# Gate functions and products ranked ahead of weight conversions, and six low-word conversions on GpSimd

## The chip, the cores and the metric

The kernel runs on one core of a Trainium2 chip. The metric is the device time of one execution in microseconds (us), the median of several runs. The engines are PE (TensorE matmuls), PEld (its weight loads), DVE (VectorE), ACT (ScalarE), POOL (GpSimd) and SP (SyncE, which here issues DMAs); each executes its own queue of instructions strictly in order, and engines wait for each other by semaphores.

## The reference

Two stages in float32. First a linear recurrence over 768 steps for 4 batches and 8 heads of size 48, then a feed-forward network over the 3072 tokens with 384 channels and 2048 hidden units, whose gate is Mish:

```python
def _attn_ref(r, k, v, w, u):
    for t in range(S):
        cur = np.einsum('bhd,bhe->bhde', u[None] * kt, vt)
        y[:, :, t] = np.einsum('bhd,bhde->bhe', rt, state + cur)
        state = w[None, :, :, None] * state + np.einsum('bhd,bhe->bhde', kt, vt)

def _moe_ref(x, w_in, w_out):
    h = x @ w_in
    sp = np.where(h > 20.0, h, np.log1p(np.exp(np.minimum(h, 20.0))))
    g = h * np.tanh(sp)
    return g @ w_out
```

The recurrence's output, with heads side by side, is x. The two weights arrive as 64-bit floats and have to be turned into 32-bit ones on the chip.

## The kernel before

**Work and tiles.** The recurrence is computed in 24 steps (s = 0 to 23), each a chunk of 64 time steps for two batches. A step scales its r and k (L484, L540), forms scores on PE (L555), masks them with `copy_predicated` (L595), multiplies with v (L608, or L621 in later steps) and keeps a state (L663, copied out by L679). A step yields one slice of x, 128 tokens wide: for the first steps it is transposed on PE (L750), copied out of PSUM by ACT (L719), and from group 1 on a rest is taken by DVE (L722).

The feed-forward network goes over 8 groups of three slices (384 tokens). In each group there are 16 hidden tiles of 128 units, 0 to 15. A tile has an up product (`hp`), which is copied out of PSUM to `hb` (L918), a gate, and a down product into three accumulators (`acc`). Four tiles form a batch for the gate. Its functions work on all four tiles at once on ACT: sigmoid (L835), arctan (L838) and sine (L841), the first and the last behind a load of a function table (ACT_TABLE_LOAD). The products with `hb` follow on DVE in two halves (L850). Group 0 uses whole float32 weights (L811, L824, L869); from group 1 on x, gate and weights are each split into a rounded part and a rest, with three matmuls for one (L777; L853 and L856 split the gate, L384 and L386 the weights).

**Weights.** Each of the two weights arrives in eight loads of 768 KB, numbered 0 to 15 in the order of use (`W_ORDER`). Load 7, for instance, holds the up weights of tiles 10 and 11, load 9 those of tiles 12 and 13, load 10 the down weights of tiles 6 and 7. A load is converted in place once, in group 0's time: its low words are turned into a small float by `convert_low` (L341, ACT); its high words go through an absolute value (L358 on ACT or L360 on DVE), a clamp (L362), a shift (L364), a merge with the sign (L367) and an integer add of both words (L369), which ends the conversion (event `whole`). The buffer `we` between them has two slots.

**What sets the order.** All of this is written as generators ("threads") that yield the engines that could do the next operation with an estimated price, or the name of an event to wait for. The planner `Flow.run` takes at each step the engine and the thread that can start first by these estimates, and among those that can start at the same time the one of the lowest rank. The instructions are then issued in just this order (`manual_schedule`), so each engine's queue is fixed at build time. Ranks are counted in hidden tiles: a thread that belongs to tile n has the rank n minus a lead. The leads are the constants `L_...`: L_IN and L_OUT for conversions of up and down weights, L_GATE for a gate's functions and the halves of its product, L_FIN for a slice's way into x. The recurrence's first steps have ranks far below all others. In the first 30 us PE gets dummy matmuls (L285) to keep its clock up.

## Time and profile before

| | us |
|---|---|
| median of 3 runs | 525.7 |
| lowest, highest run | 525.6, 526.51 |
| profiled execution, its own time | 524.44 |
| span of the profile (first to last instruction) | 522.7 |
| busy in the span: PE, PEld | 506.4, 468.7 |
| busy in the span: ACT, DVE, GpSimd | 402.3, 321.4, 10.1 |
| mean granted TensorE clock | 0.994 |

A row of the profile gives the line, the engine, the operation and the tiles written and read (out<-in), with busy time, mean time of one instruction in nanoseconds, and the idle time ahead of it with its cause. In the order of time the first two columns are start and length in us. A group's float32 matmul of the whole weights counts as two instructions.

### The profile page before, as it was taken

How to read it: one execution, taken by the hardware profiler on the slowest of the kernel's cores; microseconds unless marked ns; L12 is line 12 of the kernel's file. 1: busy time of each engine (PE TensorE's matmuls, PEld its weight loads, DVE VectorE, ACT ScalarE, POOL GpSimd, SP SyncE). 2: the span in 40 equal slices, each digit the busy share in tenths (PEclk: the TensorE clock that was granted, in tenths of full speed). 3: DMA queues.
4: the chain of work that ended last, by engine and by line, in shares of the span. 5: the costliest groups of instructions: out<-in, count | busy, mean ns of one | idle time of the engine just before them, and what ended most of it. 6: DMA issues, size and time to landing. Idle time of an engine off the chain costs nothing.

```text
span 522.7 us, 11439 instructions
## 1 busy us (share of the span) xinstructions
PE 506.4 (97%) x4757; PEld 468.7 (90%) x4757; DVE 321.4 (62%) x486; ACT 402.3 (77%) x505; POOL 10.1 (2%) x23
## 2 busy tenths in 40 slices
PE   8797999999999999999999999999999999999994
PEld 6674666788999999999999999999999999999994
DVE  7989889857775475565564475575474473334341
ACT  6889985968988778667787678667687767777883
POOL 7000000000000000000000000000000000000000
PEclk9998999999999999999999999999999999999998
DMA  8998444323333343423533343413343240001001
GB/s 256 415 376 266 113 117 119 95 56 107 90 110 107 96 141 100 113 63 93 148 91 87 98 134 100 107 52 105 113 126 96 70 153 15 2 1 45 2 0 51
DMA packets 31051, 57.88 MB, mean 111 GB/s; under 512 B 6064, under 2 KB 19248, under 8 KB 30992
## 3 DMA queue, kind: packets, MB, share of 16 engines
q1 hardware_dynamic: 27536, 52.32, 34.1%
q10 hardware_dynamic: 3456, 4.75, 2.6%
q8 instruction: 39, 0.64, 0.5%
q14 instruction: 20, 0.16, 0.1%
HBM read 36.80 MB, written 4.72 MB: 79 GB/s over the span
## 4 chain that ended last, share of the span: by engine, by line
PE 84%; ACT 6%; DVE 3%; DMA 2%; issue 2%; SPq 2%; ACTq 0%
PE hp L777 30%; PE acc L777 28%; PE acc L869 6%; PE pa L555 5%; PE hp L824 5%; PE yt L621 3%; PE st L663 3%; PE yt L608 1%; SPq L742 1%; PE hp L811 1%; ACT L841 1%; ACT fa L841 1%; ACT fa L838 1%; DMA rk<-in_rkT_dram 1%; DVE rk L484 1%
## 5 line engine op out<-in xcount | busy, mean ns | idle before, releaser
L777 PE MATMUL hp<-x,w 128*128 128x384 f32 x1008 | 197.2, 338 | 0.5 <-DMA x<-rkn 0.5
L777 PE MATMUL acc<-gh,w 128*128 128x384 f32 x672 | 187.9, 335 | 1.0 <-ACT gh L853 1.0
L777 PEld LDWEIGHTS hp<-x,w 128*128 128x128 f32 x1008 | 175.7, 188 | 3.7 <-issue 0.7
L777 PEld LDWEIGHTS acc<-gh,w 128*128 128x128 f32 x672 | 122.8, 188 | 1.4 <-ACT gh L853 1.3
L777 PE MATMUL acc<-gl,w 128*128 128x384 f32 x336 | 112.3, 334 | 0.2 <-DVE gl L856 0.2
L918 ACT COPY hb<-hp 128x384 f32<-128x384 f32 x104 | 49.2, 474 | 55.5 <-PE hp L777 47.2
L850 DVE TENSOR_TENSOR hb<-hb,fa 128x768 f32<-128x768 f32 (+1 forms) x58 | 51.8, 927 | 41.0 <-ACT fa L841 40.9
L853 ACT CAST gh<-hb 128x768 fp32r<-128x768 f32 (+1 forms) x58 | 47.2, 816 | 22.2 <-DVE hb L850 22.0
L777 PEld LDWEIGHTS acc<-gl,w 128*128 128x128 f32 x336 | 63.1, 188 | 0.4 <-DVE gl L856 0.4
L918 DVE COPY hb<-hp 128x384 f32<-128x384 f32 x24 | 13.4, 556 | 77.6 <-PE hp L777 77.4
L856 DVE TENSOR_TENSOR gl<-hb,gh 128x768 fp32r<-128x768 f32 (+1 forms) x58 | 52.7, 929 | 7.7 <-ACT gh L853 5.9
L835 ACT ACTIVATE fa<-hb,bias_ln 128x1536 f32<-128x1536 f32 (+1 forms) x33 | 50.9, 1542 | 0.4
L838 ACT ACTIVATE fa<-fa 128x1536 f32<-128x1536 f32 (+1 forms) x33 | 47.8, 1449 | 1.9 <-ACT ob L881 1.7
L841 ACT ACTIVATE fa<-fa 128x1536 f32<-128x1536 f32 (+1 forms) x33 | 47.8, 1448 | 0.4
L841 ACT ACT_TABLE_LOAD x33 | 42.3, 1283 | 0.6
L835 ACT ACT_TABLE_LOAD x33 | 42.3, 1283 | 0.6
L869 PE MATMUL acc<-g,wraw 128*128 128x384 f32 x96 | 35.6, 509 | 3.4 <-issue 3.4
L484 DVE TENSOR_TENSOR rk<-rk,TRK 112x1024 f32<-112x1024 f32 x23 | 28.3, 1236 | 15.7 <-DMA rk<-in_rkT_dram 15.7
L869 PEld LDWEIGHTS acc<-g,wraw 128*128 128x128 f32 x96 | 19.0, 204 | 14.0 <-issue 5.2
L555 PE MATMUL pa<-rk 48*64 48x64 f32 x736 | 26.4, 221 | 1.7 <-DVE gl L595 1.7
L555 PEld LDWEIGHTS pa<-rk 48*64 48x64 f32 x736 | 23.2, 134 | 4.5 <-DVE gl L595 2.0
L824 PE MATMUL hp<-x,wraw 128*128 128x384 f32 x78 | 27.0, 490 | 0.0
(91 smaller groups left out, 454.7 us busy)
## 6 DMA issues: line engine op xcount, KB each, us to landing
rk<-in_rkT_dram SPq DMA_DIRECT2D x23, 448.0 KB, 4.0
rkn<-in_rkN_dram SPq DMA_DIRECT2D x18, 384.0 KB, 4.0
wraw<-in_w_in_dram SPq DMA_DIRECT2D x8, 768.0 KB, 12.3
wraw<-in_w_out_dram SPq DMA_DIRECT2D x8, 768.0 KB, 15.6
G<-rk SPq DMA_DIRECT2D x36, 128.0 KB, 2.3
Wt<-in_vN_dram SPq DMA_DIRECT2D x46, 96.0 KB, 2.8
out_dram<-ob ACTq DMA_DIRECT2D x23, 192.0 KB, 2.3
G<-rk SPq DMA_DIRECT2D x42, 96.0 KB, 2.4
```

Of the source, the lines that this page charges most:

```text
L484: nc.vector.tensor_tensor(out=rk[:112], in0=rk[:112], in1=TRK[:112].unsqueeze(2).broadcast_to([112, 2, 2, NP, C]), op=ALU.mult)
L555: nc.tensor.matmul(pa[TROWS[par], n : n + C], lhsT=keys[r, c, p, :], rhs=rk[r, 0, c, p, :], start=True, stop=True)
L777: nc.tensor.matmul(out, lhsT=a, rhs=m, start=first and n == 0, stop=last and n == 2)
L824: nc.tensor.matmul(hp[:, :T], lhsT=w[:, fs], rhs=o.x[:, 0, k, :T], start=k == 0, stop=k == KT - 1)
L835: nc.scalar.activation(o.g, o.hb, AF.Sigmoid, bias=bias_ln2, scale=1.0)
L838: nc.scalar.activation(o.g, o.g, AF.Arctan)
L841: nc.scalar.activation(o.g, o.g, AF.Sin, scale=2.0)
L850: nc.vector.tensor_tensor(out=to[:, j], in0=o.hb[:, j], in1=o.g[:, j], op=ALU.mult)
L853: nc.scalar.copy(out=o.gh[:, j], in_=o.hb[:, j])
L856: nc.vector.tensor_tensor(out=o.gl[:, j], in0=o.hb[:, j], in1=o.gh[:, j].bitcast(F32), op=ALU.subtract)
L869: nc.tensor.matmul(accs[mt][:, :T], lhsT=w[:, ws], rhs=o.gh[:, j], start=first, stop=last)
L918: (nc.scalar.copy if engine == "act" else nc.vector.tensor_copy)(out=o.hb[:, j], in_=h)
```

## The change

Two edits. The lead of a gate's functions and products, L_GATE, goes from 2 tiles to 5, so that in the planner they rank ahead of conversions of the same and of some later tiles. And the conversion of low words may go to GpSimd, at an estimated 1.8 us, where the planner finds that this ends sooner.

```diff
-L_ATT, L_V, L_IN, L_OUT, L_GATE, L_EVAC, L_PUT, L_FIN = 4, -2, 2, 4, 2, 12, 9, 4
+L_ATT, L_V, L_IN, L_OUT, L_GATE, L_EVAC, L_PUT, L_FIN = 4, -2, 2, 4, 5, 12, 9, 4
@@ def convert_low(c):
         yield f"raw{c}"
         low = raws[c][:, :, 0]
-        yield act(WE)
-        nc.scalar.activation(low.bitcast(F32), low, AF.Copy, bias=2.0, scale=2.0**-51)
+        engine = yield {**act(WE), "pool": 1.8}
+        if engine == "act":
+            nc.scalar.activation(low.bitcast(F32), low, AF.Copy, bias=2.0, scale=2.0**-51)
+        else:
+            nc.gpsimd.tensor_scalar(
+                out=low.bitcast(F32), in0=low, scalar1=2.0**-51, scalar2=2.0, op0=ALU.mult, op1=ALU.add
+            )
         flow.set(f"low{c}")
```

The lines behind the second edit move down by five (L369 becomes L374, L824 becomes L829). The planner gives six of the sixteen conversions to GpSimd: loads 2, 3, 9, 11, 12 and 14. Ahead of the first stands a library instruction on GpSimd, and the memset of `ones`, which the check of the decay's range needs on PE, stands behind the second. On the other engines the order changes from 20 us on; three places matter here. The names `wraw_N` are weight loads, `hp_N` up products, `g_N` gate products, all numbered anew in each build.

ACT, from the copy of tile 3 to the end of batch 0's sine. Before:

```order
L918 COPY hb_573<-hp_597 128x384
L341 ACTIVATE wraw_584<-wraw_584 128x768
L835 ACT_TABLE_LOAD
L835 ACTIVATE fa_620<-hb_573,bias_ln2_76 128x1536
L918 COPY hb_609<-hp_623 128x384
L838 ACTIVATE fa_620<-fa_620 128x1536
L341 ACTIVATE wraw_603<-wraw_603 128x768
L918 COPY hb_609<-hp_633 128x384
L841 ACT_TABLE_LOAD
L841 ACTIVATE fa_620<-fa_620 128x1536
```

And in the changed kernel:

```order
L923 COPY hb_576<-hp_597 128x384
L840 ACT_TABLE_LOAD
L840 ACTIVATE fa_613<-hb_576,bias_ln2_76 128x1536
L342 ACTIVATE wraw_604<-wraw_604 128x768
L923 COPY hb_607<-hp_621 128x384
L843 ACTIVATE fa_613<-fa_613 128x1536
L923 COPY hb_607<-hp_632 128x384
L846 ACT_TABLE_LOAD
L846 ACTIVATE fa_613<-fa_613 128x1536
```

One conversion (of load 9) has left this stretch for GpSimd; that of load 10 has moved ahead of the arctan.

DVE, around the conversion of load 7 (`wraw_534` before, `wraw_536` now; `we_649` and `we_659` are its buffer). Before, from batch 0's product on:

```order
L850 TENSOR_TENSOR g_654<-hb_573,fa_620 128x768 x2
L362 TENSOR_SCALAR we_665<-we_665 128x768
L367 SCALAR_TENSOR_TENSOR we_649<-wraw_534,we_649 128x768
L364 TENSOR_SCALAR we_665<-we_665 128x768
L369 ISA wraw_534<-wraw_534,we_649 128x768x2
L484 TENSOR_TENSOR rk_553<-rk_553,TRK_105 112x1024
L540 TENSOR_TENSOR rkn_675<-rkn_675,TKn_106 128x384
L484 TENSOR_TENSOR rk_684<-rk_684,TRK_105 112x1024
L540 TENSOR_TENSOR rkn_692<-rkn_692,TKn_106 128x384
```

And in the changed kernel, where `g_720` is batch 1's product:

```order
L489 TENSOR_TENSOR rk_559<-rk_559,TRK_105 112x1024
L545 TENSOR_TENSOR rkn_679<-rkn_679,TKn_106 128x384
L489 TENSOR_TENSOR rk_690<-rk_690,TRK_105 112x1024
L545 TENSOR_TENSOR rkn_698<-rkn_698,TKn_106 128x384
L923 COPY hb_682<-hp_705 128x384
L510 TENSOR_TENSOR gl_183<-rk_690,uw_114 112x512
L374 ISA wraw_569<-wraw_569,we_662 128x768x2
L855 TENSOR_TENSOR g_720<-hb_607,fa_675 128x768
L600 COPY_PREDICATED gl_184<-cst_70,pa_721 128x512
L855 TENSOR_TENSOR g_720<-hb_607,fa_675 128x768
L600 COPY_PREDICATED gl_184<-cst_70,pa_738 128x512
L374 ISA wraw_536<-wraw_536,we_659 128x768x2
```

The last step of load 7 (L369, now L374) stood right behind batch 0's product and now stands behind batch 1's.

PE, at the end of group 0, from tile 15's up product (`hp_1104`, `hp_1101`) to the first of group 1 (`hp_1135`, `hp_1141`). Before:

```order
L824 MATMUL hp_1104<-x_427,wraw_617 128x384 x3
L750 MATMUL t_1116<-cst_70,G1_81 128x128 x3
L869 MATMUL acc0_669<-g_925,wraw_630 128x384
L869 MATMUL acc1_671<-g_925,wraw_630 128x384
L869 MATMUL acc2_673<-g_925,wraw_630 128x384
L777 MATMUL hp_1135<-x_853,w_775 128x384 x9
```

And in the changed kernel:

```order
L829 MATMUL hp_1101<-x_428,wraw_617 128x384 x3
L874 MATMUL acc0_668<-g_977,wraw_630 128x384
L874 MATMUL acc1_670<-g_977,wraw_630 128x384
L874 MATMUL acc2_672<-g_977,wraw_630 128x384
L755 MATMUL t_1123<-cst_70,G1_81 128x128 x3
L782 MATMUL hp_1141<-x_846,w_763 128x384 x9
```

The transpose of the last slice of group 1's x has moved behind the down product, right ahead of the tile that reads this slice. ACT at the same place, in the changed kernel; before, the slice's copy (L719) stood ahead of the table load and the sigmoid:

```order
L923 COPY hb_915<-hp_1101 128x384
L389 CAST w_1118<-wraw_371 128x768
L840 ACT_TABLE_LOAD
L840 ACTIVATE fa_1120<-hb_915,bias_ln2_76 128x1536
L724 CAST x_846<-t_1123 128x3x128
```

The copy of the slice (now L724) stands behind batch 3's sigmoid.

## The prediction

> **What bounds the kernel now.** I read the page's sums first, then busy time by stage, then the chain that ended last, then the order of time around its one hole.

> ```profile
> PE 506.4 (97%) x4757; PEld 468.7 (90%) x4757; DVE 321.4 (62%) x486; ACT 402.3 (77%) x505; POOL 10.1 (2%) x23
> ```

> PE is busy for 97% of the span; a change can win only where PE does not run. GpSimd stands nearly idle.

> ```profile
> 25.00:30.00 5.00, 3.96 (x77) 3.24 (x75) 5.00 (x10) 4.90 (x11) 0.00 (x0) 1.00 1.04 337
> 45.00:50.00 5.00, 1.60 (x4) 0.79 (x3) 4.41 (x7) 4.97 (x6) 0.00 (x0) 0.88 0.94 205
> 200.00:300.00 100.00, 100.00 (x969) 98.14 (x969) 55.44 (x82) 75.28 (x88) 0.00 (x0) 1.00 0.36 101
> ```

> After the length of the stage come PE, PEld, DVE, ACT, POOL, then the granted clock. From 100 us on PE has no gap, and ACT is three quarters busy: faster conversions buy nothing there. At 25 to 50 us DVE and ACT are full, and in 45 to 50 PE works 1.60 of 5.

> ```profile
> 45.55 3.39 issue
> 48.94 3.79 PE acc L869 x6
> ...
> 54.67 1.94 PE acc L869 x6
> ```

> The chain of waits shows the hole: 3.39 us, and behind it six passes of a down product that take 3.79 us where the next six take 1.94. So the hole costs 3.4, and 1.85 more for a slow clock:

> ```profile
> 48.50:49.00 0.50, 0.06 (x1) 0.09 (x1) 0.50 (x2) 0.50 (x2) 0.00 (x0) 0.79 0.95 196
> ...
> 52.00:52.50 0.50, 0.50 (x2) 0.20 (x1) 0.50 (x2) 0.49 (x2) 0.00 (x0) 0.80 0.00 0
> ...
> 517.00:518.00 1.00, 0.18 (x2) 0.00 (x0) 0.25 (x1) 0.48 (x1) 0.00 (x0) 1.00 0.44 160
> ...
> 519.00:520.00 1.00, 0.00 (x0) 0.00 (x0) 0.00 (x0) 0.00 (x0) 0.00 (x0) 0.92 0.41 126
> ```

> The clock was halved from 48.8 to 52.2 us (0.79 and 0.80 are shares of those half microseconds). At the end PE stops at 517.2 and the clock halves at 519.84, 2.7 us later. So a wait of 2.7 us or more can be enough. What filled the hole:

> ```profile
> 37.92 0.47 ACT L918 COPY hb<-hp 128x384 f32<-128x384 f32 x1
> 38.28 0.95 ACT L341 ACTIVATE wraw<-wraw 128x768 f32<-128x768 uint32 x1
> ...
> 39.25 1.28 ACT L835 ACT_TABLE_LOAD   x1
> ...
> 40.55 1.58 ACT L835 ACTIVATE fa<-hb,bias_ln 128x1536 f32<-128x1536 f32 x1
> ...
> 42.03 0.46 ACT L918 COPY hb<-hp 128x384 f32<-128x384 f32 x1
> ...
> 42.39 1.49 ACT L838 ACTIVATE fa<-fa 128x1536 f32<-128x1536 f32 x1
> ...
> 43.78 0.91 ACT L341 ACTIVATE wraw<-wraw 128x768 f32<-128x768 uint32 x1
> ...
> 44.59 0.46 ACT L918 COPY hb<-hp 128x384 f32<-128x384 f32 x1
> ...
> 45.07 1.28 ACT L841 ACT_TABLE_LOAD   x1
> ...
> 46.36 1.49 ACT L841 ACTIVATE fa<-fa 128x1536 f32<-128x1536 f32 x1
> ...
> 47.88 1.83 DVE L850 TENSOR_TENSOR g<-hb,fa 128x768 f32<-128x768 f32 x2 [0.41 <-ACT fa L841]
> ```

> ACT runs batch 0's gate without a pause, with two conversions (L341) between; the first half of the product L850 ends near 48.8 and PE starts at 48.9. The label "issue" hides a plain wait for this chain. An instruction's successor starts about 0.09 us before its end (42.39 + 1.49 against 43.78), which I subtract below.

> **Term 1, the hole at 45.6.** GpSimd takes load 9's low words, so the L341 at 38.28 leaves the chain; load 10's stays in it. The sigmoid, arctan and sine follow 38.28 to 39.25 earlier: 0.97 us, and the sine ends at 46.85. DVE has in front of L850 in the new order the copy of tile 7, which waits for PE at 45.6 (0.47), and one conversion step (0.88): 46.95. PE starts at 47.95 instead of 48.91: **-1.0**. A wait of 2.4 us is shorter than 2.7, so I let the clock stay: **-1.85**. If it drops all the same, PE is later and the next wait shorter by as much.

> **Term 2, a new wait at tile 10.** Load 7 (weights of tiles 10 and 11) loses its rank.

> ```profile
> 51.43 0.95 DVE L369 CUSTOM_DVE_ANT_0 wraw<-wraw,we 128x1536 uint16<-128x1536 uint16 x1
> ...
> 62.52 2.10 PE L824 MATMUL hp<-x,wraw 128*128 128x384 f32 x6
> ```

> Before, its last step ends at 52.4 and PE uses it at 62.5. In the new order that step stands behind the products of batch 1 and both masked copies. Those products wait for batch 1's sine. From the start of batch 0's sine (45.35) ACT runs: sine, two L358, one L341, table, sigmoid, L341, copy, arctan, four L503, table, sine.

> ```profile
> L595 DVE COPY_PREDICATED gl<-cst,pa 128x512 f32<-128x512 uint32 x12 | 8.8, 734 | 1.4 <-PE pa L555 1.4
> L341 ACT ACTIVATE wraw<-wraw 128x768 f32<-128x768 uint32 x16 | 14.4, 928 | 0.0
> L358 ACT ACTIVATE we<-wraw 128x768 f32<-128x768 f32 x9 | 8.4, 930 | 2.1 <-DVE wraw L369 2.1
> L503 ACT ACTIVATE gl<-rk,uw 112x128 f32<-112x128 f32 x20 | 6.4, 392 | 0.0
> ```

> 1.49 + 2 x 0.93 + 0.93 + 1.28 + 1.58 + 0.93 + 0.47 + 1.49 + 4 x 0.39 + 1.28 + 1.49 = 14.4, less 13 overlaps of 0.09: 13.2. The sine ends at 58.6. Then DVE: product 0.92, masked copy 0.73, product 0.92, masked copy 0.73, last step 0.95, less four overlaps: 3.9, so 62.5, and PE can start tile 10 at 62.6. PE's work before it is the same as before: 62.52 - 48.94 = 13.58, less 1.85 of slow clock, is 11.73; from 47.95 it is there at 59.7. Wait: **+2.9**. Terms 1 and 2 together leave PE at tile 10 where it was, at 62.6. A second slice's four L503 have become one DVE product ahead of these five; DVE waits for the sine there anyway, so I cost it at nothing, and 0.7 without that cover. Behind tile 10 PE holds the products of slice 3; SP places their input from the second masked copy, which ends a microsecond earlier, so they come hardly later. SP's own queue keeps its order but for swaps of neighbouring pairs: nothing.

> **Term 3, a new wait at the first tile of group 1.** Before, the transpose of the last slice of x stands ahead of a down product, and its copy (L719) ahead of batch 3's sigmoid:

> ```profile
> 94.88 0.49 PE L750 MATMUL t<-cst,G 128*128 128x128 f32 x3
> ...
> 95.46 0.48 ACT L719 CAST x<-t 128x384 fp32r<-128x384 f32 x1
> ...
> 96.02 0.55 DVE L722 TENSOR_TENSOR x<-t,x 128x384 fp32r<-128x384 f32 x1
> ...
> 96.86 1.32 PE L777 MATMUL hp<-x,w 128*128 128x384 f32 x5
> ```

> Down product and slice run side by side, and PE does not wait. In the new order the down product comes first, then the transpose, then at once the tile that needs the slice; on ACT the table load and sigmoid of batch 3 stand ahead of the copy. From the end of tile 15: PE 1.94 + 0.49 = 2.4, then it waits. ACT: 0.2 until the copy starts, copy 0.47, L384 (like L341) 0.93, table 1.28, sigmoid 1.58, slice 0.48, less 0.4, then L722 0.55 and 0.1 of handing over: 5.2. Wait: **+2.8**.

> **Term 4, the clock.** Two waits of 2.8 to 2.9 lie between 2.7 (dropped at the end) and 3.4 (dropped at 48.8); each can cost from 0 to 1.85. I take one drop, begun inside its wait, so partly free: **+1.6**; ends 0 and 3.7. [...]

> **Term 5, GpSimd.** Six conversions of 768 elements go to it, behind a library instruction that the trace of before does not show. Nearest rows:

> ```profile
> 6.15 0.50 POOL L295 COPY KI<-KI 48x384 f32<-48x384 f32 x1 [0.46 <-ACT KI L265]
> 7.33 1.55 POOL L295 COPY KI<-KI 48x384 f32<-48x384 f32 x1 [0.68 <-ACT KI L265]
> ...
> 10.63 0.75 DVE L540 TENSOR_TENSOR rkn<-rkn,TKn 128x384 f32<-128x384 f32 x1
> ...
> L540 DVE TENSOR_TENSOR rkn<-rkn,TKn 128x384 f32<-128x384 f32 x24 | 13.3, 557 | 0.0
> ```

> A copy of 384 took 0.50 alone, 1.55 beside a DVE product, and another made a DVE product 0.2 longer. Twice the elements: 1.0 to 3.1 for GpSimd, 0 to 1.0 for DVE each. The result is needed late:

> ```profile
> 21.45 0.92 ACT L341 ACTIVATE wraw<-wraw 128x768 f32<-128x768 uint32 x1
> ...
> 30.68 0.94 DVE L369 CUSTOM_DVE_ANT_0 wraw<-wraw,we 128x1536 uint16<-128x1536 uint16 x1
> ```

> Load 2 is there by 21.45 and used at 30.68; a slow conversion, the library instruction and the range check's `ones`, now queued behind two conversions, hide in these 9 us. The price is what DVE loses at 19 to 27 us, where it is full:

> ```profile
> 24.93 0.41 DVE L468 COPY G<-gl 64x512 f32<-64x512 f32 x1
> ...
> 25.40 0.47 ACT L679 COPY Wt<-st 48x384 f32<-48x384 f32 x1
> ```

> PE's next step waits for both; DVE is there at 25.34, ACT at 25.87: 0.5 of cover. Two conversions at 0.4 each (twice the 0.2): 0.8 - 0.5 = **+0.3**; ends 0 and 2 x 1.0 - 0.5 = 1.5. Later losses fall into term 1 and come off term 2. The 0.92 us that ACT saves six times is worth nothing beyond term 1.

> **Sum.** -1.0 - 1.85 + 2.9 + 2.8 + 1.6 + 0.3 = +4.75 on the profiled execution's 524.44 us (span 522.70), 529.2. The median of the runs, 525.7, lies 1.3 above that execution; on it 530.4, which I predict.

> **Rivals.** (a) Faster: only the hole counts. Both new waits come from order, but need ACT and DVE as slow as in these rows; if batch 1's sine ended by 55.6 instead of 58.6 and the slice came 2.8 us sooner, the gain stands alone: 525.7 - 2.85 = 522.9. For it: the chain's hole is real. Against: ACT has no pause from 38 to 51 us. (b) One of the two new waits is there, the other hidden: -2.85 + 2.9 = 0, so 525.8, or 527.4 with a clock drop. (c) GpSimd shuts DVE out for its whole operation: each conversion 1.8 (the price in the change) to DVE, 2 x 1.8 - 0.5 = 3.1 in place of 0.3: 533.2. For it: the 1.55 against 0.50. Against: L540 lost only 0.2. [...] (d) GpSimd's share changes nothing: then terms 1 to 4 stand, 530.1. (e) The clock drops in neither new wait: 530.4 - 1.6 = 528.8; the tail's 2.7 us speak against it, the waits' being under 3.4 for it.

> **Chances.** My forecast, (d) with it, 0.54 and (e) 0.25, (a) 0.05, (b) 0.10, (c) 0.06. Within 0.2% is 1.05 us, about what a measurement of this kernel can tell. Faster: (a) and a little of (b), 0.07; same: most of (b), 0.07; slower 0.86. The range: lowest main case without clock drop and GpSimd's price on the profiled execution's base, 527.3; highest with two drops and 1.5 at the front, 525.7 + 2.85 + 3.7 + 1.5 = 533.75. I give 527.0 to 533.8.

> **What would show it.** Right: the first hole down to about 2.4 us at a down product; a wait of about 3 us ahead of tile 10's up product, released by the last step of load 7 on DVE; one of about 2.8 ahead of group 1's first tile, released by L722's new line; PE without gap from 100 us. Wrong: no wait at tile 10, or GpSimd's conversions over 3 us with DVE's instructions beside them twice as long.

## The result and the profile after

The changed kernel takes 531.82 us (median of 6 runs, 529.86 to 532.92), the kernel before beside it 525.75: a ratio of 1.0107, 95% interval 1.0086 to 1.0128, or 5.6 us slower (the two medians lie 6.1 apart). 530.4 was predicted, with a range of 527.0 to 533.8. The profiled execution took 532.92 us (span 531.1), the longest of the six; what goes with the 3 us between executions is told in the last section. The ratios leave out two executions far off all others, one of 1729.34 us in the fifth experiment and one of 717.61 of the kernel before beside the last three.

The first line is the page's row of TensorE and the rest, then come the waits of PE from 40 to 120 us after the change (waited for, total us, times, longest); before it there was one, of 3.4 us.

```profile
PE 511.9 (96%) x4757; PEld 472.2 (89%) x4757; DVE 322.7 (61%) x485; ACT 398.6 (75%) x497; POOL 17.4 (3%) x29
...
PE acc L874 <- issue: 3.7, 1, 3.7
PE hp L782 <- ACT x L724: 2.4, 1, 2.4
PE hp L829 <- DVE wraw L374: 1.8, 1, 1.8
PE hp L782 <- DVE x L727: 0.2, 1, 0.2
```

PE's busy time grew by 5.5 us with the same 4757 instructions. The clock is halved in three stretches of 3.41 us more than before (below); half their length, 5.1 us by estimate, is nearly all of it. The hole is still there, and the two new waits are those forecast, with the releasers that were forecast: load 7's last step (L374) and the last slice's copy (L724, then L727). In the timeline of PE they stand so:

```profile
50.62 3.69 PE L874 MATMUL acc<-g,wraw 128*128 128x384 f32 x6 [3.65 <-issue]
...
66.11 2.21 PE L829 MATMUL hp<-x,wraw 128*128 128x384 f32 x6 [1.85 <-DVE wraw L374]
...
103.37 0.44 PE L782 MATMUL hp<-x,w 128*128 128x384 f32 x1 [2.36 <-ACT x L724]
```

The clock, by stretches of 3.41 us cut where it changed (PE's busy time is the second number, the granted clock the third from the end):

```profile
12.72:16.14 3.42, 1.61 (x37) 1.29 (x36) 3.41 (x7) 2.28 (x6) 0.00 (x0) 1.00 1.02 411
16.14:19.55 3.41, 3.41 (x66) 3.22 (x61) 3.33 (x7) 2.85 (x4) 0.00 (x0) 0.50 1.01 416
19.55:22.96 3.41, 3.41 (x66) 2.91 (x66) 2.49 (x3) 1.74 (x5) 1.95 (x3) 0.50 1.02 417
...
50.27:53.68 3.41, 3.06 (x5) 1.85 (x6) 3.41 (x7) 3.33 (x4) 0.00 (x0) 0.50 0.19 59
...
63.92:67.34 3.42, 1.57 (x6) 0.85 (x5) 3.42 (x6) 0.94 (x1) 0.00 (x0) 1.00 0.25 57
101.47:104.88 3.41, 1.36 (x6) 1.10 (x7) 3.09 (x6) 3.39 (x4) 0.00 (x0) 1.00 0.29 87
104.88:108.30 3.42, 3.42 (x9) 2.41 (x8) 1.69 (x3) 3.39 (x3) 0.00 (x0) 0.50 0.24 58
```

Four stretches are halved: two at the front, one behind the hole, one behind the wait at group 1; none behind tile 10. The front pair is not the change's doing: the profile of the rank alone (first experiment), which has the order of before up to group 1, shows it as well (a clock of 0.50 from 16.66 to 23.48 us), and the profile of before does not (1.00 from 11.25 to 21.49). So I compare landmarks with that profile where I can. Where PE's work starts at three landmarks, and where it ends, in us:

| kernel | first down product | tile 10 | group 1 | PE's end |
|---|---|---|---|---|
| before | 48.94 | 62.52 | 96.86 | 517.18 |
| rank alone | 50.45 | 64.11 | 98.45 | 518.52 |
| after | 50.62 | 66.11 | 103.37 | 525.19 |

Against the rank alone the changed kernel loses 0.17 us up to the first down product, 1.83 to tile 10 (the wait of 1.85), 2.92 to group 1 (the wait of 2.36, and 0.56 because PE's own passes from tile 15 to there, in their new order, take 4.47 in place of 3.91), and 1.75 behind it, all of it busy time (the halved stretch): 6.67 in all.

Why did the hole not shrink? DVE's instructions between 34 and 52 us, grouped by shape (count, busy us, mean ns); the conversion steps that met GpSimd, first after the change, then before:

```profile
L374 DVE CUSTOM_DVE_ANT_0 wraw<-wraw,we 128x1536 uint16<-128x1536 uint16 x4 | 4.4, 1114 | 0.0
L372 DVE SCALAR_TENSOR_TENSOR we<-wraw,we 128x768 uint32<-128x768 uint32 x4 | 4.3, 1122 | 0.0
L367 DVE TENSOR_SCALAR we<-we 128x768 f32<-128x768 f32 x5 | 3.3, 688 | 0.0
L365 DVE TENSOR_SCALAR we<-wraw 128x768 uint32<-128x768 uint32 x3 | 2.3, 772 | 0.0
```

```profile
L369 DVE CUSTOM_DVE_ANT_0 wraw<-wraw,we 128x1536 uint16<-128x1536 uint16 x5 | 4.8, 956 | 0.0
L367 DVE SCALAR_TENSOR_TENSOR we<-wraw,we 128x768 uint32<-128x768 uint32 x4 | 3.8, 954 | 0.0
...
L362 DVE TENSOR_SCALAR we<-we 128x768 f32<-128x768 f32 x5 | 2.8, 554 | 0.1
...
L360 DVE TENSOR_SCALAR we<-wraw 128x768 uint32<-128x768 uint32 x2 | 1.1, 560 | 0.0
```

The same steps are longer by 4 x 0.158 + 4 x 0.168 + 5 x 0.134 + 3 x 0.212 = 2.6 us. Four GpSimd conversions run in this stretch: 0.65 us of DVE for each. Three timeline views of the changed kernel, of GpSimd, ACT and DVE, show one collision and the end of the chain; the last row is DVE in the rank alone:

```profile
19.95 0.89 POOL L344 TENSOR_SCALAR wraw<-wraw 128x768 f32<-128x768 uint32 x1 [7.37 <-DMA wraw<-in_w_in_dram]
...
36.39 1.45 POOL L344 TENSOR_SCALAR wraw<-wraw 128x768 f32<-128x768 uint32 x1 [13.48 <-DMA wraw<-in_w_in_dram]
...
46.86 1.48 ACT L846 ACTIVATE fa<-fa 128x1536 f32<-128x1536 f32 x1
...
36.13 2.51 DVE L372 SCALAR_TENSOR_TENSOR we<-wraw,we 128x768 uint32<-128x768 uint32 x2
...
49.58 1.81 DVE L855 TENSOR_TENSOR g<-hb,fa 128x768 f32<-128x768 f32 x2
...
49.39 1.83 DVE L855 TENSOR_TENSOR g<-hb,fa 128x768 f32<-128x768 f32 x2 [0.44 <-ACT fa L846]
```

A conversion takes 0.89 us at its shortest. The one at 36.39 lasts 1.45, and the two DVE steps beside it 2.51 instead of 1.81 (0.954 each, an overlap of 0.09). The first of them takes its usual 0.95, so the second has some 1.65: the lengths fit a conversion that waits for the first step to end, and a second step that waits for the conversion. Batch 0's sine is done at 48.34, but its product starts at 49.58, because DVE is still at its conversions. In the rank alone the sine ends at 49.35 and DVE stands waiting for it, from 49.39 at its product. So ACT did get done 1.0 us sooner, and DVE lost that again: the chain that PE waits for now ends on DVE.

### The profile page after: what moved, and what is told of

It is laid out like the page before. It is cut to its first block, busy times and chain, and to the rows that moved or that the text cites. A ratio compares the mean times of both kernels' runs of the same rounds, so it can differ in the third digit from the quotient of the medians.

```text
span 531.1 us, 11471 instructions
## 1 busy us (share of the span) xinstructions
PE 511.9 (96%) x4757; PEld 472.2 (89%) x4757; DVE 322.7 (61%) x485; ACT 398.6 (75%) x497; POOL 17.4 (3%) x29
## 3 DMA queue, kind: packets, MB, share of 16 engines
q10 hardware_dynamic: 3456, 4.75, 2.5%
## 4 chain that ended last, share of the span: by engine, by line
PE 88%; ACT 5%; DVE 3%; issue 1%; DMA 1%; SPq 0%; ACTq 0%
PE hp L782 33%; PE acc L782 30%; PE acc L874 6%; PE pa L560 5%; PE hp L829 5%; PE yt L626 4%; PE st L668 3%; PE hp L816 1%; PE yt L613 1%; DMA rk<-in_rkT_dram 1%; ACT fa L840 1%; ACT L840 1%; ACT L846 1%; ACT fa L846 1%; ACT fa L843 1%
## 5 line engine op out<-in xcount | busy, mean ns | idle before, releaser
L923 ACT COPY hb<-hp 128x384 f32<-128x384 f32 x104 | 49.3, 474 | 65.6 <-PE hp L782 52.4
L923 DVE COPY hb<-hp 128x384 f32<-128x384 f32 x24 | 13.3, 556 | 89.7 <-PE hp L782 87.8
L861 DVE TENSOR_TENSOR gl<-hb,gh 128x768 fp32r<-128x768 f32 (+1 forms) x58 | 52.2, 928 | 2.4 <-ACT gh L858 0.8
L874 PE MATMUL acc<-g,wraw 128*128 128x384 f32 x96 | 36.7, 521 | 3.7 <-issue 3.7
L829 PE MATMUL hp<-x,wraw 128*128 128x384 f32 x78 | 27.1, 492 | 1.8 <-DVE wraw L374 1.8
```

The source lines that it names most:

```text
L829: nc.tensor.matmul(hp[:, :T], lhsT=w[:, fs], rhs=o.x[:, 0, k, :T], start=k == 0, stop=k == KT - 1)
L861: nc.vector.tensor_tensor(out=o.gl[:, j], in0=o.hb[:, j], in1=o.gh[:, j].bitcast(F32), op=ALU.subtract)
L874: nc.tensor.matmul(accs[mt][:, :T], lhsT=w[:, ws], rhs=o.gh[:, j], start=first, stop=last)
L923: (nc.scalar.copy if engine == "act" else nc.vector.tensor_copy)(out=o.hb[:, j], in_=h)
```

## The experiments

Two theories were put up. Theory 1: the loss lies in the order, and passes through the waits at tile 10 and group 1. Theory 2: it lies in DVE's time beside GpSimd's conversions. Ratios are to the kernel before on the same chip, whose median was 526.35 us beside experiments 1 to 4, 526.43 beside 5 to 8 and 526.26 beside 9 to 11. Differences in us are worked out from the ratios.

**1. The rank alone** (e1).

```diff
-L_ATT, L_V, L_IN, L_OUT, L_GATE, L_EVAC, L_PUT, L_FIN = 4, -2, 2, 4, 2, 12, 9, 4
+L_ATT, L_V, L_IN, L_OUT, L_GATE, L_EVAC, L_PUT, L_FIN = 4, -2, 2, 4, 5, 12, 9, 4
```

> Only the rank of gate functions and products goes from 2 to 5; every low-word conversion stays on ACT. In the order of the instructions nothing differs from the kernel before until group 1, since what waits for a gate function ahead of that is its input and not its rank; behind it a few pieces on DVE and ACT trade places at 100 us and later, where PE has no gap. Theory 1 (the time goes through two waits of PE that the new order makes, at tile 10 and at group 1's first tile): neither wait is there, so 525.7 us, 524.7 to 526.7. Theory 2 (the time goes because DVE is held up beside GpSimd's conversions): the same 525.7. If the rank by itself moved the slice behind the gate, the wait at group 1 would be there: 528 to 530.

Measured: 525.31 us, ratio 0.9983 (0.9969 to 0.9997). The first half of the change moves by itself nothing where PE waits, and costs nothing.

**2. GpSimd in the old order** (e2): the conversion of loads 2, 3, 9, 11, 12 and 14 is written for GpSimd without the planner knowing.

```diff
-        nc.scalar.activation(low.bitcast(F32), low, AF.Copy, bias=2.0, scale=2.0**-51)
+        if c not in (2, 3, 9, 11, 12, 14):
+            nc.scalar.activation(low.bitcast(F32), low, AF.Copy, bias=2.0, scale=2.0**-51)
+        else:
+            nc.gpsimd.tensor_scalar(out=low.bitcast(F32), in0=low, scalar1=2.0**-51, scalar2=2.0, ...)
```

> The kernel before in its own order, with the low words of loads 2, 3, 9, 11, 12 and 14 converted on GpSimd at the same places, and nothing else. The profile of the changed kernel shows DVE's instruction beside such a conversion about 0.68 us longer, six times. Theory 1: no new wait at tile 10 or group 1; loads 2 and 3 make DVE 1.4 us late at 20 to 25 us and loads 9 and 11 make it late for the first product, while ACT's chain starts earlier; together 0 to 1.5 us slower: 526.5 (525.0 to 527.5), with the one hole at 46 us 3 to 4 us long. Theory 2: all six collisions are paid on the path, 6 x 0.68 = 4.1 us: 529.8 (528.5 to 531).

Measured: 527.77 us, ratio 1.0022 (1.0005 to 1.0040), 1.2 us slower: theory 1's figure, not theory 2's. (The trace of the changed kernel shows five collisions, not six: the one DVE step beside the conversion at 21.84 us takes 0.96, and elsewhere 0.95.) The view of the conversion's line (ns: least, median, most) and the longest of PE's waits at 12 to 120 us:

```profile
L344 POOL TENSOR_SCALAR wraw<-wraw x6: 900/1210/1728, 19.5 to 44.1; 128x768 f32<-128x768 uint32 x6
...
PE acc L874 <- issue: 4.3, 1, 4.3
```

The one wait between the front and 120 us is the hole, 4.3 us long: freeing ACT of six conversions made it longer, since DVE was late (the sine ends at 48.47, the product starts at 49.76). Behind it the clock is halved for two stretches, 49.68 to 56.50, where before had one; so a part of the 1.2 us is the clock's.

**3. The new order with all conversions on ACT** (e3): in the changed kernel the planner still counts them on GpSimd, but they are written for ACT.

```diff
-        if engine == "act":
+        if True:
             nc.scalar.activation(low.bitcast(F32), low, AF.Copy, bias=2.0, scale=2.0**-51)
```

> Every instruction in the changed kernel's order, but the six conversions of GpSimd are put on ACT at the places that they have in it. Theory 1: the waits at tile 10 and at group 1's first tile are there as before the edit, and ACT, which is without a pause at 38 to 58 us, has 0.92 us more for each conversion ahead of the first gate and the second: hole, tile 10 and one wait ahead of it together 3 to 5 us longer, 534.5 us (532 to 537). Theory 2: with no conversion on GpSimd DVE loses nothing, and the time falls back to 525 to 527.

Measured: 532.34 us (531.46 to 536.62), ratio 1.0125 (1.0092 to 1.0159). Theory 2 wanted 525 to 527 and falls; theory 1's 534.5 is 2 us too high, and its range of 532 to 537 just holds the result. The longest waits of PE at 40 to 200 us (the profiled execution took 535.96 us, 3.6 above the median):

```profile
PE hp L829 <- DVE wraw L374: 3.8, 1, 3.8
PE acc L874 <- issue: 3.3, 1, 3.3
PE hp L782 <- ACT x L724: 2.4, 1, 2.4
```

With no conversion on GpSimd the order still brings both new waits; the one at tile 10 is twice as long, and ACT now has the conversions in its chain for batch 1. The interval overlaps that of the changed kernel (1.0086 to 1.0128): in this order it makes no measurable difference which engine converts these six.

**4. GpSimd offered to the planner, the rank left at 2** (e4). Against the changed kernel:

```diff
-L_ATT, L_V, L_IN, L_OUT, L_GATE, L_EVAC, L_PUT, L_FIN = 4, -2, 2, 4, 5, 12, 9, 4
+L_ATT, L_V, L_IN, L_OUT, L_GATE, L_EVAC, L_PUT, L_FIN = 4, -2, 2, 4, 2, 12, 9, 4
```

> The planner may use GpSimd, as in the change, but the rank of the gate stays 2. In the order PE's, ACT's and DVE's rows up to tile 15 are nearly those of the changed kernel (load 7's last step behind the products of batch 1), but the last slice of x stands ahead of batch 3's sigmoid, as before the change. Theory 1: the wait at tile 10 stays (about 2 us), the one at group 1 with the clock drop behind it goes (2.9 + 1.7): 528 us (526.0 to 530.0). Theory 2: the six conversions are all still there, so the time is that of the changed kernel, 531 to 532.5.

Measured: 528.19 us, ratio 1.0041 (1.0026 to 1.0057), 2.2 us slower. PE's waits at 40 to 200 us, and its timeline ahead of group 1:

```profile
PE acc L874 <- issue: 3.6, 1, 3.6
PE hp L829 <- DVE wraw L374: 1.8, 1, 1.8
PE hp L782 <- DMA x<-rkn: 1.0, 2, 0.5
...
99.24 0.49 PE L755 MATMUL t<-cst,G 128*128 128x128 f32 x3
99.57 2.11 PE L874 MATMUL acc<-g,wraw 128*128 128x384 f32 x6
101.22 2.02 PE L782 MATMUL hp<-x,w 128*128 128x384 f32 x9
```

Tile 10 still waits 1.8. At group 1 the transpose (L755) stands ahead of the down product, as before the change, and the wait is gone. So the offer of GpSimd moves load 7, and only offer and rank together move the slice: from this run to the changed kernel the ratio grows by 0.0066, 3.5 us. That is less than the 2.9 and 1.75 read off above, and the third row says why in part: with PE earlier at group 1, it waits 1.0 us at 160 to 180 us for a slice that comes by DMA, where the changed kernel loses 0.05.

**5 and 6. The kernel before with its hole filled** (e5), **and the gap at 13 us as well** (e6). Both add passes of zeros that real passes overwrite.

```diff
+        if o.whole and mt == 0:              # e5 and e6, ahead of the first down product
+            for _ in range(24):
+                nc.tensor.matmul(accs[0][:, :256], lhsT=zeros[:, :128], rhs=zeros, start=True, stop=True)
...
+        if s == 1: keep_warm(10)             # e6 alone, ahead of the second block of scores
```

> The kernel before, and ahead of the first pass of the first down product 24 passes of zeros into the sum's own bank, 0.121 us each (14 took 1.70 in the trace), 2.9 us in all, inside the hole of 3.4 that PE spends waiting for the first product; the first real pass overwrites them. Theory 1 (a clock drop behind a hole is paid with half of the work in its 3.4 us, 1.85 us before the change): no halved stretch at 48 to 52 us, 523.9 us against 525.7, a ratio of 0.9965 (0.995 to 0.998). Rival (the clock drop costs nothing, because PE would wait later for ACT and DVE instead): the ratio is 1.000, and a new wait of 1.5 to 1.9 us stands between 50 and 70 us.

> As the run before it, and 10 more passes of zeros (1.2 us) ahead of the second block of scores, in the gap of 1.7 us at 13 us. In the profiles of the changed kernel and of the rank alone two windows behind this gap are at half clock (16 to 23 us) and the hole at 46 us ends 1.5 to 1.7 us later than in the profile of before, which has no such stretch. Theory 1: the front drop comes in about half of the executions and costs 1.5 us there, so the median falls by another 0.7 us, 523.2, ratio 0.995 (0.993 to 0.997), and the runs lie closer together than the 4 us of before. Rival: the front has slack, ratio as without these ten.

Measured: e5 524.06 us, ratio 0.9958 (0.9942 to 0.9975): 2.2 us faster than before, with no new wait. PE's timeline, then the stretch behind the hole with its clock:

```profile
46.16 2.78 PE L871 MATMUL acc<-zeros 128*128 128x256 bf16 x24
49.70 2.21 PE L874 MATMUL acc<-g,wraw 128*128 128x384 f32 x6 [0.75 <-DVE g L855]
...
51.30:54.71 3.41, 3.41 (x12) 2.03 (x11) 3.41 (x6) 3.38 (x4) 0.00 (x0) 1.00 0.00 0
```

The wait is now named after the product, and the clock stays whole: 2.2 us (1.3 to 3.1) agrees with the price of 1.85 for a drop. e6 is a miss: 526.07 us, ratio 0.9987 (0.9971 to 1.0003), 1.5 us slower than e5, though the two intervals still touch. Its two longest waits at 12 to 120 us say where:

```profile
PE st L668 <- issue: 2.3, 1, 2.3
PE yt L613 <- issue: 1.2, 1, 1.2
```

PE stands twice with nothing to wait for, 3.4 us in all; before the change the stops there took 0.93 and 1.04. The passes behind the gap take 1.15 to 1.24 us for 32, as before the change (up to 1.95 in e5, where the clock is 0.50 from 17.16 to 20.58), but behind the longer stop the clock is 0.50, from 31.70 to 35.11 us. What holds PE there no row says, and no run tried it by itself.

**7. The changed kernel with its two waits filled** (e7): the 24 passes as above, and 16 into the bank of group 1's first tile.

```diff
         hp = ps.tile([128, 512], F32, name="hp", tag="hp", bufs=2)
+        for _ in range(16 if not o.whole and f == 0 and o.x is xs[1] else 0):
+            nc.tensor.matmul(hp[:, :256], lhsT=zeros[:, :128], rhs=zeros, start=True, stop=True)
```

> The changed kernel with the same 24 passes in its hole at 47 us and 16 passes of zeros (1.9 us) in the wait at group 1's first tile, into that tile's own bank. PE waits as long as before for its real work. Theory 1: neither wait is followed by a halved stretch; 1.85 and 1.7 us are gone of the clock's price and the rest of the loss stays: 531.8 - 3.5 = 528.3 (527.0 to 530.0), a ratio of 1.005 to the kernel before. Rival (the loss is all wait, the clock no part of it): 531 to 532.5, ratio 1.010.

Measured: 529.79 us, ratio 1.0073 (1.0049 to 1.0096), against 1.0107: 1.8 us less where 3.5 were expected, and the two intervals overlap. The profile shows a whole clock behind the hole (1.00 from 50.75 to 54.17 us) and from 110 to 200 us, and where the rest went. First its longest waits at 40 to 200 us, then the stretch from 160 to 170 us of this kernel and of the changed one:

```profile
PE hp L829 <- DVE wraw L374: 2.1, 1, 2.1
PE acc L874 <- DVE g L855: 0.8, 1, 0.8
PE hp L782 <- ACT x L724: 0.6, 1, 0.6
PE hp L782 <- DMA x<-rkn: 0.5, 1, 0.5
PE hp L782 <- issue: 0.4, 1, 0.4
```

```profile
160.00:170.00 10.00, 9.05 (x51) 8.36 (x50) 5.45 (x8) 8.78 (x11) 0.00 (x0) 1.00 0.43 106
```

```profile
160.00:170.00 10.00, 9.95 (x58) 9.66 (x57) 6.35 (x11) 8.33 (x13) 0.00 (x0) 1.00 0.33 75
```

At tile 10 PE waits 2.1 instead of 1.85, and at 160 to 170 us, where group 2's slice comes by DMA, it loses 0.95 us, of which the changed kernel loses only 0.05. Over all runs the mean granted clock rose from 0.9887 in the changed kernel to 0.9948, by estimate 0.0061 x 529 = 3.2 us of clock, of which 1.8 arrived. So a part of the clock's price behind group 1 was covered by that later wait; I had priced it as if nothing stood behind it.

**8. Load 7 ahead of batch 1's products** (e8), in the changed kernel:

```diff
         n = -(-o.n // GS)
+        if b == 1:
+            yield "whole7"
```

> The changed kernel, but the products of batch 1 are offered to the planner only once load 7 is whole, so its last step stands ahead of them on DVE. From there on the planner's order moves too: two blocks of PE's work between tiles 10 and 13 trade places, and the gates of batches 2 and 3 start a little earlier. Theory 1 (the wait at tile 10 is for that step): the wait of 1.9 us at tile 10 is gone; PE reaches group 1 so much the earlier or waits there for the last slice by as much as it gained. If the slice comes early enough, 528.5; if PE only waits later, 531. I expect 529 (527 to 531), with no gap of over 1 us at 60 to 70 us. Rival (PE there waits for something else, the tiles' copies or batch 1's gate): the gap at tile 10 stays at 1.5 to 2 us and the time at 531 to 532.5.

Measured: 529.24 us, ratio 1.0061 (1.0038 to 1.0083), as expected. PE's waits at 40 to 200 us:

```profile
PE acc L874 <- issue: 3.3, 1, 3.3
PE hp L782 <- ACT x L724: 1.2, 1, 1.2
PE t L755 <- ACT G L699: 0.6, 1, 0.6
```

No wait at 60 to 70 us: it was load 7's step. Of group 1's wait 1.8 us are left, in two pieces (98.9 and 100.7 us). No run takes both new waits away at once.

**9 and 10. The gate put ahead by hand, without GpSimd** (e9), **and what is left of the hole filled** (e10). In the kernel before the conversions of loads 9 and 10 are written behind batch 0's sine, load 6's last step and load 7's shift behind its products; e10 adds 16 passes of zeros.

```diff
-            nc.scalar.activation(low.bitcast(F32), low, AF.Copy, bias=2.0, scale=2.0**-51)
+            later("a" if c in (9, 10) else "", lambda: nc.scalar.activation(low.bitcast(F32), low, ...))
...
         act3(o)
+        [f() for f in held.pop("a", ()) if b == 0]
```

> The kernel before with four instructions written later, and nothing else moved: the conversions of loads 9 and 10 on ACT stand behind batch 0's sine instead of ahead of its table load and behind its arctan, and load 6's last step and load 7's shift on DVE stand behind batch 0's products. All on ACT and DVE, PE's order is that of before, no GpSimd. So the gate function does take rank here. Theory 1 (ahead of 66 us ACT and DVE set the pace, so a shorter hole comes back as a later wait): the hole falls from 3.4 to about 2.5 us, and where PE transposes the slice after next, at 66 us, it then waits 1.6 us for its copies from ACT, which come behind the moved conversions; with a clock drop as before 526.5, without 525: ratio 1.000 (0.997 to 1.003). Rival (the hole is the loss, as the change's purpose has it): -1.0 for the hole and up to -1.85 for the clock, 523 to 524.7, ratio 0.996.

> The run before it with 16 passes of zeros (1.9 us) in the hole that is left, so that the clock stays. Theory 1: PE waits at 66 us instead; equal to the kernel before with its hole filled or a little slower, ratio to before 0.996 to 1.000, and not below that run's 0.9958 by a measurable amount. Rival: 1 us better than that run, ratio 0.994 or less.

Measured: e9 525.16 us, ratio 0.9979 (0.9967 to 0.9991); e10 524.85 us, 0.9973 (0.9958 to 0.9988). The two longest waits of PE in e9 at 40 to 200 us:

```profile
PE acc L874 <- issue: 2.5, 1, 2.5
PE t L755 <- ACT G L699: 1.2, 1, 1.2
```

The hole is 0.9 us shorter, and 1.2 us come back at 69 us, where the copies of a slice stand behind the moved conversions. In this profile the six passes behind the hole take 2.18 us, against 3.69 in the changed kernel's halved stretch, so the clock did not drop there; over all runs the mean granted clock is 0.9939 against 0.9921 before: by estimate 0.0018 x 525 = 0.95 us, nearly the 1.1 gained. Filling the rest (e10) is no better than e5, their intervals overlap. Both fit theory 1: ahead of 66 us ACT and DVE set the pace, and a shorter hole is handed back.

**11. Hole filled, load 9 alone on GpSimd** (e11): as e5, and as the second experiment with another list.

```diff
-        if c not in (2, 3, 9, 11, 12, 14):
+        if c != 9:
```

> The kernel before with its hole filled by 24 passes, and the low words of load 9 alone on GpSimd, all else in the order of before. In the run with six conversions in the old order load 9's stood at 34.7 us, where DVE had a pause, took 0.90 us and cost DVE nothing. Theory 1 (a GpSimd conversion costs DVE 0.7 us only if they overlap): this one takes 0.9 to 1.0 us, no DVE instruction beside it is longer than elsewhere, ACT's gate starts 0.85 us sooner and the first product 0.4 sooner, since DVE then sets its start: 523.7, ratio 0.995 (0.993 to 0.997). Rival (GpSimd's conversion delays DVE wherever it runs): equal to the filled kernel or slower, 0.996 to 0.999.

Measured: 524.15 us, ratio 0.9955 (0.9940 to 0.9969): not to be told from e5. GpSimd's one conversion, and the DVE step beside it:

```profile
35.36 1.14 POOL L344 TENSOR_SCALAR wraw<-wraw 128x768 f32<-128x768 uint32 x1 [22.89 <-DMA wraw<-in_w_in_dram]
...
35.77 1.14 DVE L369 TENSOR_SCALAR we<-we 128x768 uint32<-128x768 uint32 x1
```

They met after all: 1.14 us where that step takes 0.55 elsewhere. What I expected of DVE did not happen, and the run says nothing on a conversion that meets no one. e5 and e11 beat both kernels.

## Why the prediction was right, step by step

The direction, the two waits and their releasers were right, and 531.82 is 1.4 us above the 530.4 named. But the closeness is in part luck: term 1 was wrong by 3.0 us, and term 2 by 1.1 the other way; the first of the signs that were to show it right, a hole down to 2.4 us, did not come. Measured against the rank alone, whose front is that of the profiled execution, the terms make 6.67 where the sum says 4.75:

- **Term 1, the hole (-1.0): it grew by 0.17.** The step that failed is "DVE has in front of L850 in the new order the copy of tile 7 and one conversion step: 46.95". It had four collisions with GpSimd behind it and came to the product at 49.58, 1.24 us after the sine. The chain on ACT did gain what the term says: 48.34 against 49.35 in the rank alone. No run takes the collisions alone out of this order, so their part in the hole is read from the trace.
- **Term 1, the clock behind the hole (-1.85): it dropped again**, at 50.27, since the hole stayed. The price agrees with e5, but it is not fixed: behind the hole the views show no halved stretch (e9, whose hole is 2.5 us), one (before, after, e1) or two (e2, e4).
- **Term 2, tile 10 (+2.9): 1.85.** The wait and its cause are shown by e8. That terms 1 and 2 together would leave PE where it was is wrong by 2.0 us: PE came there 3.0 us later than forecast, but load 7's last step was late too, by 2.1 (it ended at 66.06; the forecast's 62.5 and the front's 1.5 make 64.0).
- **Term 3, group 1 (+2.8): 2.9** between tile 10 and group 1, 2.36 of it a wait. e4 shows that it needs both halves of the change, which the order had not told me.
- **Term 4, one more drop (+1.6): 1.75**, but behind a wait of 2.4 us, which I had held to be too short. e7 gets back less than that, since a later wait covers part of it. "From 100 us on PE has no gap" was read off 200 to 300 us; before the change PE loses 0.43 us at 160 to 180 already, waiting for a slice.
- **Term 5, GpSimd (+0.3): mis-sized.** 0.4 for each collision is 0.65, and the four ahead of the first product cost more than the two I priced at the front. In the old order all six cost 1.2 us (0.3 to 2.1), net of what ACT saves (e2).

Of the rivals, (a) and (b) are out: both waits are there. So are (d), since the collisions kept the hole, and (e), since the clock dropped behind one new wait. (c), that GpSimd shuts DVE out, was right in kind and wrong in price. I had set the row of L540, 0.2 us longer, against it; the rows above show more. A DVE step that meets a conversion takes 0.65 us longer in the changed kernel, 0.59 in e11, not the 1.8 of the change's price table. Of DVE's copies out of the tiles' sums (PSUM) none stands beside a conversion in the changed kernel; in e2 one does, wholly (40.81 to 41.36, in the first of two conversions that run from 40.32 to 42.88), and takes its usual 0.55:

```profile
40.81 0.55 DVE L923 COPY hb<-hp 128x384 f32<-128x384 f32 x1
```

## What to carry to other kernels

Offering a planner one more engine can change far more of its order than the six instructions that move: build the new order with the old engines, and the old order with the new engine, and time both, before a word is said on the engine. A hole in TensorE is worth its length only if nothing behind it is late; here 0.9 us less of hole gave back 1.2 at 69 us (e9), while two dozen passes of zeros in the same hole kept the clock and gave 2.2 us. And here each conversion moved to GpSimd cost VectorE some 0.65 us where the two met, against 0.89 for the conversion at its shortest; the one copy out of PSUM that ran beside a conversion took its usual 0.55 us.
